# A convolution with two expert layers: the rest of x turned by ScalarE, late masks in PSUM, a new order for the start, and 27 matmuls that nobody reads

## The chip, the core and the metric

The kernel runs on one core of one Trainium2 chip. Time is device microseconds (us) of that core, from a run's start to its end. TensorE is called PE, VectorE DVE, ScalarE ACT, GpSimd POOL and SyncE SP, as in the profile.

## The reference

An x of 2 x 4096 tokens and 192 channels passes through a convolution over 7 tokens, whose weights are a softmax made for each token and head, and then through two layers of the same form.

```python
w = softmax(weight_gen)                       # over the 7 taps, 8 heads
x = einsum('bshk,bskhg->bshg', w, windows(x)) # 8192 tokens x 192
h = x @ moe_w_in                              # 192 x 2048
x = where(h > 0, h, exp(min(h, 0)) - 1) @ moe_w_out      # 2048 x 192
h = x @ moe2_w_in
out = (h * clip(h + 3, 0, 6) / 6) @ moe2_w_out
```

## The kernel before

**Cells.** The 8192 tokens are 16 blocks of 512. For each layer and block the 2048 hidden channels are done in 8 cells of 256, so there are 256 cells, in a fixed order. Cell n has a first product (18 matmuls into the two PSUM banks `hset[n % 2]`) and a second product (into `acca` and `accb`) that is issued three cells later, together with the first product of cell n + 3. Each operand is held as a high part and a rest, so that three products of float32r matmuls (high by high, high by rest, rest by high) stand for one exact product. Most matmuls use 64 of the 128 rows, and two of them run side by side.

**What feeds PE.** Between a cell's first and second product ACT computes relu and exp (`x n`, `y n` in the script below, for the two banks), DVE computes the gate (`X n`, `Y n`), ACT rounds the result to its high part (`R n`), and DVE makes its rest `gl` (`G n`). The operand x of a block is transposed by PE, cast by ACT to `X["h"]` (tile xh), and DVE subtracts to get `X["l"]` (tile xl). Each 64-row half of xh and xl is needed in the other half of the partitions as well. For block 0 ACT copies xh across (`turn`, written `wh2` and `wh3`), and two DMAs on SP copy xl across (`swap`).

**Weight units.** The first layer's weights arrive in 16 units of 128 x 384, `i0` to `i7` for the inner product and `o0` to `o7` for the outer, numbered 0 to 15 as in `units`. A unit k is split into high part and rest by a chain: ACT takes the absolute value into a mask (`B k`), DVE does five steps (`C k.0` to `C k.4`), ACT casts the high part (`H k`), PE sums the parts with four matmuls (`P k`: twice line 191, lines 192 and 193), and ACT casts the sum into the rest (`L k`). The string `masks` says where the mask of a unit lies: x is `aux`, b `accb`, a `acca[0]`, c `acca[1]`, all PSUM; a dash is the SBUF tile tr. The string `sums` says which PSUM bank `P k` writes (d to g are the banks of `hset`).

**Order.** Every engine works its queue in program order. From cell 0 to cell 9 the program order is written out by hand in `SCRIPT`; besides the tokens above, `M n` is cell n on PE, `s1a` to `s1c` and `e1` are the softmax of block 1, `sA`, `sE`, `sB`, `sC` that of block 2, `T1` the transposes of block 1, `J` and `j` its casts and rests, and `wl0`, `wl1` the rests of block 0. POOL multiplies and adds the seven taps of a block once its softmax is there; for block 2 it starts behind `sC` and `T1`. From cell 10 on a planner places the second layer's units by due cells. The cells and their work stay in the same order relative to each other.

Of the kernel before, what the change touches and what calls it, by code (L numbers as in the profile page):

```python
# [8 lines left out]
F32 = mybir.dt.float32  # L9
# [8 lines left out]
def kernel(  # L18
# [20 lines left out]
    nc = tc.nc  # L39
# [18 lines left out]
    UN = 2 * D  # L58
    half = slice(0, HP), slice(HP, P)
# [10 lines left out]
    hset = [[psp.tile([P, 512], F32, name=f"h{i}{k}") for k in range(2)] for i in range(2)]  # L70
# [4 lines left out]
    plus, minus = (cpool.tile([P, P], F32R, name=n) for n in ("plus", "minus"))  # L75
# [6 lines left out]
    WI = [{k: cpool.tile([P, NQ * UN], F32R, tag=f"wi0{k}", name=f"wi0_{k}") for k in "hl"}, None]  # L82
# [245 lines left out]
    def prepare(m, i):  # L328
        X = xts[m, i] = {
            k: act.tile([P, 2, XN], F32R, tag=f"x{k}", name=f"x{k}") for k in "hl"}  # L330
        v = lambda t: t[:, 0].rearrange("p (h c) -> p h c", h=2)
        if m == 0:

            y, yd = ya.pop(i)
            ps = acca if i == 0 else (acca[i % 2], aux)
            for t, src in enumerate([y[:, t, 0:P] for t in range(TM)] + [yd[:, s] for s in range(2)]):
                for h, p in enumerate(half):
                    nc.tensor.transpose(ps[h][:, t * HP:(t + 1) * HP], src[p], ident[p, p])  # L338
            parts = [(ps[h][:, 0:XN // 2], (lambda h: lambda t: v(t)[:, h])(h)) for h in range(2)]
        else:  # L340
            parts = [(zin.pop(i)[:, 0:XN], lambda t: t[:, 0])]

        def cast(k):
            src, w = parts[k]
            nc.scalar.copy(w(X["h"]), src)  # L345

        def turn(a):
            nc.scalar.copy(X["h"][half[1 - a], 1], X["h"][half[a], 0].bitcast(F32))

        def rest(k):  # L350
            src, w = parts[k]
            nc.vector.tensor_tensor(w(X["l"]), src, w(X["h"]).bitcast(F32), op=ALU.subtract)

        def swap(keys, put):
            for k in keys:
                for a in range(2):
                    put(X[k][half[1 - a], 1].bitcast(F32), X[k][half[a], 0].bitcast(F32))

        def split():
            for k in range(len(parts)):  # L360
                cast(k)
            for k in range(len(parts)):
                rest(k)
            swap("hl", lambda o, t: later(1 if (m, i) == (0, 2) else 2, o, t))
        split.cast, split.turn, split.rest, split.swap = cast, turn, rest, swap
        return split

# [144 lines left out]
    def matmuls(n):  # L512

        if n >= len(cells):
            if n - LAG < len(cells):
                whole_second_product(n - LAG)
            return  # L520
        b0, b1, a0, a1 = (second_product(n - LAG, k, b) for b in (1, 0) for k in range(2))
        gg.pop(n - LAG, None)
        l0, l1 = first_product(n, 0), first_product(n, 1)
        x1 = first_product(n + 1, 1)[:2] if n >= EARLY - 1 else []
        l1 = l1[2:] if n >= EARLY else l1
        if n < BOOT:
            rows = [(0, a0), (6, b0), (10 if n >= LAG else 0, l0)], [(0, l1), (9, a1), (15, b1), (19, x1)]
            if n >= EARLY:
                rows = rows[0], [(0, l1), (7, x1), (9, a1), (15, b1)]
        else:  # L530
            rows = [(0, b0), (4, a0), (10, l0)], [(0, l1), (7, b1), (11, x1), (13, a1)]
        plan = [
            (s + j, k, op) for k, runs in enumerate(rows) for s, ops in runs for j, op in enumerate(ops)]
        seen = [added.pop(i) for i in range(3, NB) if n == prep[0, i] - 1]
        for _, k, (o, w, r, st, sp, wait, tell) in sorted(plan, key=lambda e: e[:2]):
            mm = nc.tensor.matmul(o, w, r, start=st, stop=sp).ins  # L536
            if wait:
                tc.add_manual_dep(mm, told[wait].name, SYNC)
            elif seen and k and not tell and o in acca:
                tc.add_manual_dep(mm, seen.pop().name, SYNC)  # L540
            if tell:
                note = nc.sync.nop().ins
                tc.add_manual_dep(note, mm.name, SYNC)
                told[tell] = note
                if now > 2 and tell[1] == 1:

                    transfers(1 + k + (now < NQ))
# [47 lines left out]
    def later(n, out, in_):  # L595

        if now is None or now >= len(cells) or now < BOOT and n == 0:
            nc.sync.dma_start(out, in_)
        else:
            waiting.append((now + n, out, in_))  # L600

    def transfers(count):
        for _ in range(count):
            k = next((k for k, w in enumerate(waiting) if w[0] <= now), None)
            if k is None:
                return
            nc.sync.dma_start(*waiting.pop(k)[1:])

    class Stream:
# [21 lines left out]
    BOOT = 10  # L631
    units = [(u[0], 0, int(u[1]), k) for k, u in enumerate("i0 i1 i2 i3 o0 i4 o1 i5 o2 i6 o3 i7 o4 o5 o6 o7".split())]
    banks = {"x": aux, "b": accb, "a": acca[0], "c": acca[1], "d": hset[0][0], "e": hset[0][1], "f": hset[1][0], "g": hset[1][1]}
    masks, sums = "xxbaccxcx----ccc", "xxbfbedgfedxcxxx"
    made = {}
    SCRIPT = """
        s1a B2 B1 C2.0 e1 C1.0 wh0 s1b wh1 wh2 wl0 s1c wh3 wl1 C2.1 B4 M0 C1.1 B3 C2.2 C4.0 H2 C1.2 C4.1 H1
        C1.3 C3.0 C1.4 C4.2 P1 x0 C3.1 C4.3 C3.2 L1 M1 C4.4 y0 C2.3 X0 B5 C2.4 B6 Y0 P2 x1 C5.0 C6.0 y1 C3.3
        C6.1 X1 L2 M2 H3 C3.4 R0 Y1 C5.1 P3 H4 C6.2 x2 G0 P4 y2 C5.2 C6.3 L3 C5.3 L4 M3 C6.4 C5.4 X2 B7 B8
        Y2 R1 C8.0 C7.0 H5 C8.1 H6 P5 C7.1 x3 C8.2 G1 P6 L5 B9 B10 C7.2 L6 M4 C8.3 H7 sA C10.0 sE X3 y3 C7.3  # L640
        C10.1 C9.0 H8 C8.4 R2 C7.4 Y3 P7 x4 C9.1 C10.2 P8 C9.2 L7 G2 H10 T1 L8 C10.3 y4 M5 C9.3 X4 C9.4 J
        C10.4 sB B12 H9 j B11 R3 Y4 P9 B13 sC C11.0 C12.0 G3 P10 L9 x5 C11.1 C12.1 C11.2 L10 M6 C13.0 H11
        C12.2 C13.1 H12 C11.3 x6 C13.2 C11.4 C13.3 R4 C12.3 C13.4 P11 y5 C12.4 X5 P12 G4 H13 L11 L12 Y5 B14
        X6 M7 R5 C14.0 C14.1 x7 G5 y6 X7 C14.2 P13 H14 C14.3 Y6 L13 M8 C14.4 y7 R6 Y7 B15 G6 x8 P14 R7 C15.0
        X8 L14 M9 C15.1 C15.2 H15 C15.3 C15.4 x9 G7 y8 P15 y9 Y8 X9 L15 Y9 R8 G8
    """

    groups = [("io"[n % 2], 1, n // 2) for n in range(2 * NQ)]
# [22 lines left out]
    with tc.manual_schedule():  # L671
        nc.vector.memset(three, 3.0)
        nc.scalar.activation(warm, three, AF.Exp)
        def make(k):
            made[k] = Unit(*units[k])
# [15 lines left out]
            s()  # L691
        u.p5(aux)
        u.p6()
        for s in c0[5:]:
            s()
        c1, split = attention(1), {0: prepare(0, 0)}

        def products(n):
            nonlocal now
            if n:  # L700
                trail(n - 1)
            now = n
            if n == 2:
                blk[2] = load_block(2)
                for k in range(RAWS + 8, len(units)):
                    make(k)
            matmuls(n)
            if n == begin[2]:
                for s in softmax.pop(2):
                    s()  # L710
# [15 lines left out]
        def special(t):  # L726
            if t == "T1":
                split[1] = prepare(0, 1)
            elif t in ("s1a", "e1", "s1b"):
                c1.pop(0)()  # L730
            elif t == "s1c":
                for s in c1:
                    s()
            elif t == "J":
                split[1].cast(0)
                split[1].cast(1)
            elif t == "j":
                split[1].rest(0)
                split[1].rest(1)
                split[1].swap("hl", nc.sync.dma_start)  # L740
            elif t[:2] == "wh":
                k = int(t[2])
                (split[0].turn if k > 1 else split[0].cast)(k % 2)
            elif t[:2] == "wl":
                split[0].rest(int(t[2]))
                if t == "wl1":
                    split[0].swap("l", nc.sync.dma_start)
                    for k in range(8, RAWS + 8):
                        make(k)
            else:  # L750
                if t == "sA":
                    softmax[2] = attention(2)
                softmax[2].pop(0)()
# [6 lines left out]
        for t in SCRIPT.split():  # L760
            if t[0] == "C":
                k, p = t[1:].split(".")
                getattr(made[int(k)], "s" + p)()
            elif t[0] in plain and t[1:].isdigit():
                plain[t[0]](int(t[1:]))
            else:
                special(t)
# [65 lines left out]
```

## Time and profile before

| | us |
|---|---|
| median of the runs before | 1227.36 |
| lowest run | 1226.69 |
| the profiled execution, its own time | 1227.44 |
| its span, first to last instruction | 1225.6 |
| PE busy | 1188.1 (97%) |
| DVE busy | 944.3 (77%) |
| ACT busy | 856.4 (70%) |
| POOL busy | 417.6 (34%) |

The page of the profile gives busy time by engine. A row of the timeline gives the start in us, the duration in us, the engine, the line, the operation, output and inputs, how many instructions are merged, and in brackets the idle time in front and what ended it. A row of the windows gives the busy time of each engine in a stretch and the granted PE clock as a share of the full one.

### The profile page before, as it was taken

How to read it: one execution, taken by the hardware profiler on the slowest of the kernel's cores; microseconds unless marked ns; L12 is line 12 of the kernel's file. 1: busy time of each engine (PE TensorE's matmuls, PEld its weight loads, DVE VectorE, ACT ScalarE, POOL GpSimd, SP SyncE). 2: the span in 40 equal slices, each digit the busy share in tenths (PEclk: the TensorE clock that was granted, in tenths of full speed). 3: DMA queues.
4: the chain of work that ended last, by engine and by line, in shares of the span. 5: the costliest groups of instructions: out<-in, count | busy, mean ns of one | idle time of the engine just before them, and what ended most of it. 6: DMA issues, size and time to landing. Idle time of an engine off the chain costs nothing.

```text
span 1225.6 us, 25362 instructions
## 1 busy us (share of the span) xinstructions
PE 1188.1 (97%) x10146; PEld 941.7 (77%) x10146; DVE 944.3 (77%) x1223; ACT 856.4 (70%) x1339; POOL 417.6 (34%) x234
## 2 busy tenths in 40 slices
PE   2979999999999999999999999999999999999998
PEld 1647787777778777778788888888888888888886
DVE  7897999999999999998777666666666666666664
ACT  3858788888888888888886666556665555666654
POOL 7582778777778877777000000000000000000000
PEclk9989999999999999999999999999999999999999
DMA  9421122221122222121121111111101111111110
GB/s 207 120 63 62 40 88 89 89 79 65 39 83 89 89 88 69 41 68 53 54 64 52 28 40 53 52 40 53 46 27 46 53 53 40 53 36 30 53 40 27
DMA packets 33414, 75.42 MB, mean 62 GB/s; under 512 B 4372, under 2 KB 17042, under 8 KB 33296
## 3 DMA queue, kind: packets, MB, share of 16 engines
q1 hardware_dynamic: 33152, 73.60, 21.0%
q8 instruction: 80, 1.31, 0.5%
q14 instruction: 38, 0.31, 0.1%
q10 hardware_dynamic: 144, 0.20, 0.0%
HBM read 36.43 MB, written 12.58 MB: 40 GB/s over the span
## 4 chain that ended last, share of the span: by engine, by line
PE 91%; DVE 2%; ACT 0%; DMA 0%; issue 0%; SPq 0%
PE h L536 42%; PE acca L536 28%; PE accb L536 19%; DVE gl L567 1%; PE acca L338 1%; PE acca L432 0%; DVE r L573 0%; PE acca L504 0%; DVE boot L185 0%; PE accb L504 0%; DVE tr L174 0%; DMA xl<-xl 0%; ACT gh L563 0%; PE aux L191 0%; DVE tr L185 0%
## 5 line engine op out<-in xcount | busy, mean ns | idle before, releaser
L536 PE MATMUL h<-xl,wi_h 64*128 64x512 f32 x1536 | 563.2, 395 | 4.4 <-DMA xl<-xl 4.4
L536 PE MATMUL h<-xh,wi_h 64*128 64x512 f32 x1536 | 565.3, 396 | 2.0 <-ACT xh L345 1.5
L536 PE MATMUL h<-xh,wi_l 64*128 64x512 f32 x1536 | 567.1, 396 | 0.1
L536 PE MATMUL acca<-gh,wo 64*128 64x512 f32 x2024 | 558.3, 394 | 0.1
L567 DVE TENSOR_TENSOR gl<-r,gh 128x1024 fp32r<-128x1024 f32 x256 | 394.3, 1540 | 62.7 <-ACT gh L563 61.6
L536 PEld LDWEIGHTS acca<-gh,wo 64*128 64x128 f32 x2024 | 373.5, 185 | 48.5 <-issue 1.6
L559 ACT ACTIVATE r<-h,three 128x512 f32<-128x512 f32 x256 | 176.3, 689 | 222.2 <-PE h L536 112.4
L536 PE MATMUL accb<-gh,wo 64*128 64x512 f32 x1012 | 319.9, 395 | 0.6 <-ACT wo L198 0.6
L536 PE MATMUL acca<-gl,wo 64*128 64x512 f32 x1012 | 317.8, 393 | 1.3 <-DVE gl L567 1.2
L536 PE MATMUL accb<-gl,wo 64*128 64x512 f32 x1012 | 317.3, 393 | 0.3 <-DVE gl L567 0.3
L536 PEld LDWEIGHTS h<-xl,wi_h 64*128 64x128 f32 x1536 | 282.8, 186 | 40.1 <-DMA xl<-xl 5.1
L536 PEld LDWEIGHTS h<-xh,wi_h 64*128 64x128 f32 x1536 | 283.0, 186 | 38.9 <-ACT xh L345 1.7
L536 PEld LDWEIGHTS h<-xh,wi_l 64*128 64x128 f32 x1536 | 282.9, 186 | 35.4 <-ACT wi_l L198 0.5
L576 DVE SCALAR_TENSOR_TENSOR r<-r,h 128x512 f32<-128x512 f32 x256 | 175.8, 687 | 161.1 <-ACT r L559 160.1
L563 ACT CAST gh<-r 128x1024 fp32r<-128x1024 f32 x256 | 266.6, 1042 | 13.3 <-DVE r L573 12.5
L536 PEld LDWEIGHTS acca<-gl,wo 64*128 64x128 f32 x1012 | 186.9, 185 | 26.0 <-DVE gl L567 2.8
L536 PEld LDWEIGHTS accb<-gl,wo 64*128 64x128 f32 x1012 | 186.9, 185 | 23.8 <-DVE gl L567 0.8
L573 DVE SCALAR_TENSOR_TENSOR r<-r,h 128x512 f32<-128x512 f32 x256 | 172.9, 676 | 37.5 <-ACT r L557 36.6
L536 PEld LDWEIGHTS accb<-gh,wo 64*128 64x128 f32 x1012 | 185.0, 185 | 21.6 <-ACT wo L198 0.9
L290 POOL TENSOR_TENSOR tmp<-xt,wt 128x768 f32<-128x768 f32 (+1 forms) x95 | 189.8, 1998 | 6.2
L556 ACT ACTIVATE r<-h 128x512 f32<-128x512 f32 x256 | 152.7, 596 | 49.6 <-PE acca L536 29.0
L557 ACT ACTIVATE r<-r 128x512 f32<-128x512 f32 x256 | 162.0, 633 | 8.1
(158 smaller groups left out, 757.5 us busy)
## 6 DMA issues: line engine op xcount, KB each, us to landing
xt<-in_x_dram SPq DMA_DIRECT2D x14, 960.0 KB, 5.7
xl<-xl SPq DMA_DIRECT2D x64, 192.0 KB, 2.9
xh<-xh SPq DMA_DIRECT2D x62, 192.0 KB, 2.7
z<-z SPq DMA_DIRECT2D x16, 384.0 KB, 2.3
zin<-z SPq DMA_DIRECT2D x16, 384.0 KB, 3.0
out_dram<-ot SPq DMA_DIRECT2D x15, 384.0 KB, 2.3
raw<-in_moe_w_out_dram SPq DMA_DIRECT2D x12, 384.0 KB, 3.1
raw<-in_moe_w_in_dram SPq DMA_DIRECT2D x12, 192.0 KB, 3.4
```

Source lines behind the costliest of these rows:

```text
L290: eng.tensor_tensor(o.rearrange("p t (h g) -> p t h g", g=G), xk, wk.rearrange("p (t h) g -> p t h g", h=H), op=ALU.mult)
L338: nc.tensor.transpose(ps[h][:, t * HP:(t + 1) * HP], src[p], ident[p, p])
L536: mm = nc.tensor.matmul(o, w, r, start=st, stop=sp).ins
L556: nc.scalar.activation(r, h, AF.Relu, scale=-1.0)
L557: nc.scalar.activation(r, r, AF.Exp, scale=-1.0)
L559: nc.scalar.activation(r, h, AF.Relu, bias=three)
L563: nc.scalar.copy(gg[n][0], rs[n])
L567: nc.vector.tensor_tensor(gl, rs.pop(n), gh.bitcast(F32), op=ALU.subtract)
L573: nc.vector.scalar_tensor_tensor(r, r, -1.0, h, op0=ALU.add, op1=ALU.max)
L576: nc.vector.scalar_tensor_tensor(r, r, 6.0, h, op0=ALU.min, op1=ALU.mult)
```

## The change

Four things are edited. The two DMAs that copy the rest of x of block 0 across the partitions are replaced by two ACT copies, `wz0` and `wz1`, at places of their own in the script. The masks of units 11 and 12 move from SBUF to PSUM, 13 and 15 from `acca[1]` to `aux`; the sums of units 11 to 15 move from `aux` and `acca[1]` to banks of `hset`. The script is written anew, with the same tokens otherwise. A new function `spin` issues matmuls of 384 columns whose result nobody reads: 18 behind the sum of unit 0 and in front of block 0's transposes, 9 behind cell 0.

```diff
-        def turn(a):
-            nc.scalar.copy(X["h"][half[1 - a], 1], X["h"][half[a], 0].bitcast(F32))
+        def turn(a, k="h"):
+            nc.scalar.copy(X[k][half[1 - a], 1], X[k][half[a], 0].bitcast(F32))
...
-    masks, sums = "xxbaccxcx----ccc", "xxbfbedgfedxcxxx"
+    masks, sums = "xxbaccxcx--xcxcx", "xxbfbedgfedgfdfd"
     made = {}
     SCRIPT = """
-        s1a B2 B1 C2.0 e1 C1.0 wh0 s1b wh1 wh2 wl0 s1c wh3 wl1 C2.1 B4 M0 C1.1 B3 C2.2 C4.0 H2 C1.2 C4.1 H1
-        C1.3 C3.0 C1.4 C4.2 P1 x0 C3.1 C4.3 C3.2 L1 M1 C4.4 y0 C2.3 X0 B5 C2.4 B6 Y0 P2 x1 C5.0 C6.0 y1 C3.3
-        C6.1 X1 L2 M2 H3 C3.4 R0 Y1 C5.1 P3 H4 C6.2 x2 G0 P4 y2 C5.2 C6.3 L3 C5.3 L4 M3 C6.4 C5.4 X2 B7 B8
-        Y2 R1 C8.0 C7.0 H5 C8.1 H6 P5 C7.1 x3 C8.2 G1 P6 L5 B9 B10 C7.2 L6 M4 C8.3 H7 sA C10.0 sE X3 y3 C7.3
-        C10.1 C9.0 H8 C8.4 R2 C7.4 Y3 P7 x4 C9.1 C10.2 P8 C9.2 L7 G2 H10 T1 L8 C10.3 y4 M5 C9.3 X4 C9.4 J
-        C10.4 sB B12 H9 j B11 R3 Y4 P9 B13 sC C11.0 C12.0 G3 P10 L9 x5 C11.1 C12.1 C11.2 L10 M6 C13.0 H11
-        C12.2 C13.1 H12 C11.3 x6 C13.2 C11.4 C13.3 R4 C12.3 C13.4 P11 y5 C12.4 X5 P12 G4 H13 L11 L12 Y5 B14
-        X6 M7 R5 C14.0 C14.1 x7 G5 y6 X7 C14.2 P13 H14 C14.3 Y6 L13 M8 C14.4 y7 R6 Y7 B15 G6 x8 P14 R7 C15.0
-        X8 L14 M9 C15.1 C15.2 H15 C15.3 C15.4 x9 G7 y8 P15 y9 Y8 X9 L15 Y9 R8 G8
+        s1a B2 B1 C2.0 e1 C1.0 wh0 s1b wh1 wh2 wl0 s1c wh3 C1.1 wl1 C2.1 B3 C1.2 wz0 C3.0 C2.2 B4 C1.3 wz1
+        M0 C2.3 H1 C4.0 H2 C3.1 C4.1 x0 C1.4 C4.2 P1 C3.2 C4.3 C3.3 L1 M1 C4.4 B6 X0 B5 H3 C5.0 y0 C6.0 C5.1
+        C2.4 x1 Y0 P2 C6.1 y1 X1 C5.2 R0 C6.2 C5.3 C3.4 L2 M2 Y1 H4 H6 G0 P3 x2 P4 y2 C6.3 C5.4 L3 X2 L4 M3
+        H5 C6.4 B7 Y2 B8 sA R1 C7.0 C8.0 B10 C7.1 x3 P5 C8.1 C7.2 y3 X3 P6 G1 L5 L6 B9 H7 C7.3 M4 R2 C8.2
+        C10.0 C7.4 C9.0 C10.1 C9.1 x4 C10.2 C9.2 Y3 H8 sE C8.3 H10 P7 X4 R3 C8.4 G2 P8 L7 sB T1 L8 M5 J
+        C10.3 C9.3 sC y4 C9.4 j H9 G3 B12 B11 x5 C11.0 C10.4 Y4 P9 C12.0 P10 L9 C11.1 R4 C12.1 C11.2 C12.2
+        L10 M6 C11.3 y5 C12.3 C11.4 H11 X5 B13 Y5 x6 C12.4 C13.0 H12 P11 G4 B14 P12 L11 R5 C13.1 X6 L12 M7
+        y6 C13.2 C14.0 C13.3 x7 Y6 C13.4 H13 G5 P13 y7 C14.1 L13 X7 M8 B15 R6 C14.2 Y7 x8 C14.3 C15.0 C14.4
+        H14 G6 P14 y8 C15.1 L14 X8 M9 R7 C15.2 C15.3 Y8 x9 C15.4 G7 H15 P15 y9 X9 L15 Y9 R8 G8
     """
...
         u.p5(aux)
         u.p6()
+
+        def spin(count):
+            for _ in range(count):
+                nc.tensor.matmul(hset[1][1][:, 0:UN], plus, WI[0]["h"][:, 0:UN], start=True, stop=True)
+
+        spin(18)
         for s in c0[5:]:
...
             matmuls(n)
+            if n == 0:
+                spin(9)
...
+            elif t[:2] == "wz":
+                split[0].turn(int(t[2]), "l")
             elif t[:2] == "wl":
                 split[0].rest(int(t[2]))
                 if t == "wl1":
-                    split[0].swap("l", nc.sync.dma_start)
                     for k in range(8, RAWS + 8):
                         make(k)
```

## Rows read from the trace of the kernel before

**Rows 1.** Windows: busy us by engine, granted clock, DMA share, GB/s.
```profile
18.70:34.00 15.30, 8.50 (x34) 4.53 (x34) 11.71 (x28) 6.88 (x13) 11.52 (x9) 1.00 1.07 236
34.00:70.00 36.00, 35.17 (x237) 23.85 (x236) 34.32 (x59) 28.00 (x58) 19.48 (x12) 1.00 0.41 125
70.00:81.20 11.20, 4.00 (x8) 1.90 (x8) 11.20 (x13) 5.09 (x9) 10.73 (x7) 0.76 0.05 23
...
150.00:200.00 50.00, 50.00 (x438) 39.97 (x436) 47.26 (x56) 42.01 (x68) 40.62 (x22) 1.00 0.31 96
```

**Rows 2.** Timeline of PE, from unit 0's sum to the start of cell 2.
```profile
11.96 0.52 PE L193 MATMUL aux<-boot,plus 128*128 128x384 f32 x1
18.70 0.48 PE L338 MATMUL acca<-ident,y 64*128 64x64 f32 x4 [6.22 <-DVE y L303]
...
30.65 1.22 PE L536 MATMUL h<-xl,wi_h 64*128 64x512 f32 x4 [4.42 <-DMA xl<-xl]
...
37.64 0.33 PE L193 MATMUL accb<-boot,plus 128*128 128x384 f32 x1
37.90 0.50 PE L536 MATMUL h<-xh,wi_h 64*128 64x512 f32 x2
```

**Rows 3.** Timeline of PE, starts of cells 6 to 10 and of sums.
```profile
64.46 0.50 PE L536 MATMUL h<-xh,wi_h 64*128 64x512 f32 x1
...
76.89 0.69 PE L193 MATMUL aux<-boot,plus 128*128 128x384 f32 x1 [4.71 <-DVE boot L185]
78.97 1.65 PE L191 MATMUL acca<-f,ident 128*128 128x384 f32 x2 [1.39 <-DVE boot L185]
...
81.22 0.79 PE L536 MATMUL h<-xh,wi_h 64*128 64x512 f32 x1
...
83.08 0.49 PE L536 MATMUL h<-xh,wi_h 64*128 64x512 f32 x1
...
88.90 0.50 PE L536 MATMUL acca<-gh,wo 64*128 64x512 f32 x1
...
93.55 0.91 PE L191 MATMUL aux<-f,ident 128*128 128x384 f32 x2
...
94.74 0.50 PE L536 MATMUL acca<-gh,wo 64*128 64x512 f32 x1
...
101.27 0.49 PE L536 MATMUL accb<-gh,wo 64*128 64x512 f32 x1 [0.63 <-ACT wo L198]
```

**Rows 4.** Timeline of DVE, idle times and single steps.
```profile
23.07 0.55 DVE L352 TENSOR_TENSOR xl<-acca,xh 128x384 fp32r<-128x384 f32 x1
...
30.02 0.55 DVE L174 TENSOR_SCALAR accb<-f 128x384 uint32<-128x384 uint32 x1
33.21 0.69 DVE L573 SCALAR_TENSOR_TENSOR r<-r,h 128x512 f32<-128x512 f32 x1 [2.63 <-ACT r L557]
...
41.00 2.50 DVE L567 TENSOR_TENSOR gl<-r,gh 128x1024 fp32r<-128x1024 f32 x1
...
49.25 1.21 DVE L567 TENSOR_TENSOR gl<-r,gh 128x1024 fp32r<-128x1024 f32 x1
...
52.10 0.35 DVE L162 TENSOR_SCALAR tr<-tr 128x384 f32<-128x384 f32 x1
...
65.59 3.62 DVE L165 TENSOR_SCALAR tr<-tr 128x384 uint32<-128x384 uint32 x2
...
74.66 0.54 DVE L169 SCALAR_TENSOR_TENSOR f<-raw,acca 128x384 uint32<-128x384 uint32 x1
75.13 1.71 DVE L185 SCALAR_TENSOR_TENSOR boot<-early_l,tr 128x384 fp32r<-128x384 uint32 x1
```

**Rows 5.** Timeline of POOL, first product of block 2.
```profile
62.87 1.72 POOL L290 TENSOR_TENSOR y<-xt,wt 128x768 f32<-128x768 f32 x1 [15.89 <-PE accb L536]
```

**Rows 6.** Timeline of ACT, the two copies of xh across the partitions.
```profile
22.01 1.67 ACT L348 CAST xh<-xh 64x768 fp32r<-64x768 f32 x2
```

**Rows 7.** Windows of 2 us, the stretch behind PE's long wait.
```profile
76.00:78.00 2.00, 0.69 (x1) 0.29 (x1) 2.00 (x3) 1.67 (x4) 1.92 (x2) 0.50 0.00 0
```

## The prediction

> **What bounds the kernel now.** I read the windows first [rows 1]. From 150 us on PE is busy for all of every 50 us, with 438 matmuls in each such stretch. Nothing in the change touches that part, so it can only move as a whole: the question is how early cell 10 begins, and every us that the start saves or loses stays in the result. Cell 10 starts at 101.27 us now [rows 3].
>
> In front of that I looked for time in which PE doesn't work or works slowly. There are three places. From 18.7 to 34 us PE is busy for 8.50 of 15.3 us [rows 1]. Its timeline shows a wait of 4.42 us for the DMA of xl, with the end of cell 0 only at 30.65 + 1.22 = 31.87 us [rows 2], and DVE idle for 2.63 us as a result [rows 4]. From 34 to 70 us PE has 35.17 of 36 us and DVE 34.32 [rows 1]: both are nearly full. From 70 to 81.2 us PE has 4.00 of 11.2 us while DVE is busy throughout [rows 1]; PE waits 4.71 and 1.39 us for DVE's last step of units 11 and 12 [rows 3], and behind that the granted clock is 0.50, the lower of PE's two levels [rows 7].
>
> Why DVE is late there is seen in its own rows: two mask steps of 384 elements on the SBUF tile tr take 3.62 us at 65.59, and the last step of a unit with its mask in tr takes 1.71 us, while POOL works on block 2 from 62.87 on [rows 4, 5]. The same step without POOL takes 0.35 us, and with the mask in PSUM 0.54 us while POOL is running [rows 4].
>
> **Prices.** DVE goes from 23.07 to 30.02 us in 15 PSUM steps, so one costs 0.463 us from start to start (its duration of 0.55 overlaps by 0.09) [rows 4]. A gate, 0.69 long, then costs 0.60. A `gl` costs 2.4 us while POOL works and 1.13 without it (durations 2.50 and 1.21) [rows 4]. A last step with its mask in SBUF costs 1.63 us beside POOL, as a PSUM step without it. For softmax instructions and mask steps in SBUF without POOL I take 0.30 each (0.35 less the overlap) [rows 4]. On PE a whole cell is 93.55 - 88.90 = 4.65 us and a unit's sum 94.74 - 93.55 = 1.19 at the higher clock [rows 3]; a sum at the lower is 81.22 - 78.97 = 2.25 [rows 3]. Cells 0 to 2, with a first product alone (18 of some 39 matmuls), are half a cell, 2.3 us.
>
> **Rest of x by ScalarE.** Two turns cost 1.67 us of ACT, 0.83 each [rows 6]. They stand behind the turns of xh (which end at 23.68) and two mask openings of half as many columns. The openings are at most 0.83 each by the same row; I take 0.45. So xl is complete between 25.3 us (turns alone) and 27.0; I take 26.3. Four matmuls of cell 0 are left then, 1.22 us as before [rows 2], and cell 0 ends at 27.0 to 27.5 us instead of 31.87. SP's queue loses two DMAs that waited for DVE, so the weight loads behind them leave a little earlier. Nobody waits for those in this stretch, so I cost that at nothing.
>
> **The 18 matmuls in front.** They can start when unit 0's sum ends at 12.48 us, and PE has nothing else until 18.70 [rows 2]. Each has the shape of line 193's matmul: 0.52 us at the lower clock, 0.33 at the higher [rows 2]. That makes 5.9 to 9.4 us, an end between 18.4 and 21.9. The durations overlap, and after the wait at 78.97 the clock was back 4.1 us later (a first pair of 0.79 us at 81.22, one of 0.49 at 83.08) [rows 3], so I take an end near 18.7 and a cost of nothing. At worst the transposes come 3.2 us late. What they can give is cell 0 and unit 1 at the higher clock.
>
> **The 9 matmuls behind cell 0** take 2.7 us at the higher clock and 4.7 at the lower, from 27.0 us on. Unit 1's sum stands behind them on PE. It needs DVE's C1.4, the twelfth PSUM step after 23.07, at 28.63. So cell 1 starts at 27.0 + 2.7 + 1.2 = 30.9 and ends at 33.2. The next sum needs C2.4: 23.07 + 21 steps (9.72) + one gate (0.6) = 33.4 us. The nine are covered by this wait.
>
> **The new order, by DVE's queue.** I add up what stands in it, always with the prices above, and put PE's cells beside it.
>
> - From 33.4: three gates, five steps, `G0` beside POOL: 39.9. PE: sum 2, cell 2 at 34.6 (37.90 before [rows 2]) to 36.9, two sums, cell 3 at 39.3 to 44.0, two sums, cell 4 at 46.4.
> - Eight steps, three gates, two softmax instructions, `G1` without POOL (block 1 done): 47.1. Cell 4 wants `G1` 0.8 us after its start, so it isn't held, and ends at 51.1.
> - Seven steps, four short ones, two gates: unit 8's last step ends at 52.8 and sum 8 at 54.0; the transposes of block 1 (0.48 for four at the lower clock [rows 2]; 0.6 for twelve) follow, and cell 5 runs from 54.6 to 59.3. DVE goes on with `G2`, four softmax instructions and two short steps to 55.7. That is `sC`, and POOL starts block 2 there, not at 62.87.
> - C9.4 beside POOL 1.63, `j` 0.93, `G3` 2.4, one step, C10.4 1.63: 62.8. Sum 9 ends at 60.5 and PE waits 2.3 us for C10.4. Cell 6 starts at 64.0 against 64.46 [rows 3]. So the lead of 3.3 us at cell 2 is used up, because the work of units 11 and 12 and the softmax of block 2 also lie ahead of DVE's later steps, and DVE is the bound.
> - Three gates, nine steps: C12.4 ends at 68.7; one step and `G4`: 71.6. PE: cell 6 to 68.7, two sums, cell 7 at 71.05 instead of 81.22, to 76.05 (5.0, with matmuls of cell 8 taken in).
> - Five steps, two gates: C13.4 at 75.1; `G5`: 77.5. PE: one sum, cell 8 at 77.25 instead of 88.90 [rows 3].
> - Five steps, two gates: C14.4 at 81.0, wanted at 81.9. `G6`: 83.4, wanted at 83.85. Four steps, two gates: C15.4 at 86.5, wanted at 87.7. PE is the bound again, by 0.3 to 1.2 us.
>
> From cell 8 to cell 10 nothing differs from before (12.37 us [rows 3]), so cell 10 starts at 89.6 us, 11.6 earlier. The gain is almost all at the wait in front of cell 7 and the lower clock behind it; units 11 to 15 as PSUM masks make it.
>
> The Trainium skill speaks against this edit: "VectorE: DVE Perf Modes", section "Why PSUM operands drop a tier", says that a PSUM operand takes an fp32 instruction out of the faster two-port mode. By that alone units 11 and 12 lose three steps of 0.2 us each (0.35 against 0.55 [rows 4]), 1.2 us, and the time would be 1228.6. The rows at 65.59 and 74.66 [rows 4] decide otherwise while POOL is running. The Trainium skill's "SBUF — State Buffer", section "Who interferes with whom", has the reason: a DVE instruction with at most one SBUF input and outside that mode doesn't contend with POOL.
>
> **Sums in the banks of hset.** L11 to L14 on ACT must read them before the next cell writes there. Cell 7's first writes need L11, done 0.5 us after sum 11, and ACT has 0.6 us or more to spare; I take nothing, at most 0.5 us for each of cells 7 to 9.
>
> **The sum.** The profiled execution took 1227.44 us, 0.08 above the median of the runs. 1227.44 - 11.6 = 1215.8 us.
>
> **Rivals.** (A) POOL holds DVE longer. A hold can last one whole POOL instruction, 1.72 us [rows 5], in front of DVE's own time: 2.85 for a `gl` and 2.2 for C9.4 and C10.4. With `G3` to `G6` that is 4 x 0.45 + 2 x 0.55 = 2.9 us more, of which 0.3 is spare: 1218.4. For it speaks that POOL begins right at C9.4; against it that the `gl` at 41.00 took 2.50. (B) DVE wins at `sC` and C9.4, `G3` and C10.4 run as without POOL: 2 x 1.17 + 1.27 = 3.6 us earlier, of which PE can use the 2.3 us of its wait in front of sum 10: 1213.5. (C) The spins don't lift the clock, the change doesn't do what it says. Then the nine end at 32.2, sum 1 at 34.4, cell 1 at some 37.4, and cell 2 starts at 38.6 instead of 34.6. DVE's X1 waits for cell 1 just as long, C10.4 slips by 4.0 us, and the time is 1219.8. Against it: PE works from 12.48 without a pause, as it did when the clock came back at 83.08. (D) Slower than before: PE idles 2.3 us in front of sum 10, the clock falls there as it did by 76 to 78 us [rows 7], and the waits for `gl` in cells 6 to 9 keep it low. A cell then costs 9.3 us instead of 4.65. The return at 83.08 cost half of 4.1 us; the gain is gone when PE works over 23 us at the lower level. Against it: the wait that brought the level down was twice as long, 4.71 us.
>
> **How the numbers follow.** Chances: the forecast 0.48, A 0.20, B 0.15, C 0.12, D 0.05. A to C all lie within 1213.5 to 1219.8; with the ends of the unknown prices (the cell starts behind hset's banks, 1.5 us; the spins' lateness, of which the wait for C2.4 covers all but 1 us) the range is 1211.5 to 1221.5. A measurement of this kernel can tell 2% from no change, 24.5 us; more than that could be gained only if more than PE's two gaps went: 0.02. Within 2%: 0.94. Slower by more: 0.04.
>
> **What would show it.** In the profile after, cell 0 should end near 27 us with no wait for a DMA, its matmuls at 0.4 us; PE should wait for DVE some 2 us in front of sum 10; cell 7 should start near 71 and cell 10 near 90; no granted clock under 1 between 60 and 100 us; steps of units 11 to 15 near 0.55 us. A gain much above 14 us, or cell 10 after 95, makes this wrong.

## The result and the profile after

The changed kernel takes 1214.52 us (median; 1213.84 to 1215.17) against 1227.36 us before: a ratio of 0.9895, with a 95% interval of 0.9876 to 0.9915. One of the four runs before took 2097.70 us and is left out. A second set of runs (e12) gave 1214.11 against 1228.16, 0.9886 (0.9871 to 0.9901). So the kernel is about 1% quicker: clear of the noise, and within the 2% for which the prediction gave 0.94. The profiled execution took 1214.76 us with a span of 1213.0, so 12.7 us less than the profiled execution before. 1215.8 was predicted.

The windows after, same stretches and columns as [rows 1]:

```profile
18.70:34.00 15.30, 12.83 (x61) 8.62 (x61) 12.83 (x31) 10.90 (x20) 12.39 (x10) 0.67 1.04 283
34.00:70.00 36.00, 33.80 (x226) 23.56 (x226) 35.83 (x68) 31.27 (x64) 24.36 (x15) 1.00 0.31 99
70.00:81.20 11.20, 11.20 (x85) 8.24 (x83) 10.75 (x17) 8.65 (x17) 10.81 (x6) 1.00 0.01 2
150.00:200.00 50.00, 50.00 (x438) 39.96 (x436) 46.52 (x58) 41.05 (x67) 40.60 (x21) 1.00 0.25 72
```

From 70 to 81.2 us PE is now busy throughout, with 85 matmuls instead of 8, at a clock of 1.00 instead of 0.76. From 150 us on PE's part of the row is as before. In the first stretch PE is busier, but 9 of its 61 instructions are matmuls that nobody reads, and the clock is 0.67. The 1.00 of the same stretch before [rows 1] is no higher clock (see the last section).

PE's timeline, which answers to [rows 2, 3]: unit 0's sum, the 18, the transposes, the end of cell 0, the nine, sums 1 and 2, cell 2, sum 10, the starts of cells 6 to 10.

```profile
12.09 0.52 PE L193 MATMUL aux<-boot,plus 128*128 128x384 f32 x1
12.41 3.93 PE L697 MATMUL h<-wi_h,plus 128*128 128x384 f32 x18
18.76 0.34 PE L338 MATMUL acca<-ident,y 64*128 64x64 f32 x4 [2.42 <-DVE y L303]
...
25.81 1.22 PE L536 MATMUL h<-xl,wi_h 64*128 64x512 f32 x4 [0.19 <-ACT xl L348]
26.96 3.25 PE L697 MATMUL h<-wi_h,plus 128*128 128x384 f32 x9
30.01 1.23 PE L191 MATMUL aux<-f,ident 128*128 128x384 f32 x2
...
35.15 0.91 PE L191 MATMUL accb<-f,ident 128*128 128x384 f32 x2 [1.24 <-DVE boot L185]
...
36.34 0.50 PE L536 MATMUL h<-xh,wi_h 64*128 64x512 f32 x2
...
62.17 0.91 PE L191 MATMUL h<-f,ident 128*128 128x384 f32 x2 [0.70 <-DVE r L573]
...
63.38 0.49 PE L536 MATMUL h<-xh,wi_h 64*128 64x512 f32 x1
...
70.21 0.49 PE L536 MATMUL h<-xh,wi_h 64*128 64x512 f32 x1
...
76.50 0.49 PE L536 MATMUL acca<-gh,wo 64*128 64x512 f32 x1
...
82.34 0.50 PE L536 MATMUL acca<-gh,wo 64*128 64x512 f32 x1
...
88.88 0.50 PE L536 MATMUL accb<-gh,wo 64*128 64x512 f32 x1 [0.63 <-ACT wo L198]
```

Cell 0 ends at 25.81 + 1.22 = 27.03 us, where it ended at 31.87. But at cell 2 the lead is 37.90 - 36.34 = 1.6 us, and at cell 6 it is 1.1. Cell 7 starts at 70.2 instead of 81.2 and cell 10 12.4 us earlier than before. That is the whole difference of the spans (1225.6 - 1213.0 = 12.6) but for 0.2.

DVE's rows, which answer to [rows 4]: a wait in the new order, then the last steps of units 9 and 10 (masks in SBUF), a step of unit 11 (mask in PSUM), and the rests `gl`.

```profile
33.14 0.57 DVE L162 TENSOR_SCALAR acca<-acca 128x384 f32<-128x384 f32 x1 [2.37 <-ACT acca L158]
...
56.66 0.55 DVE L185 SCALAR_TENSOR_TENSOR boot<-early_l,tr 128x384 fp32r<-128x384 uint32 x1
...
58.07 1.64 DVE L567 TENSOR_TENSOR gl<-r,gh 128x1024 fp32r<-128x1024 f32 x1
...
60.09 1.43 DVE L185 SCALAR_TENSOR_TENSOR boot<-early_l,tr 128x384 fp32r<-128x384 uint32 x1
...
62.51 0.55 DVE L165 TENSOR_SCALAR aux<-aux 128x384 uint32<-128x384 uint32 x1
...
73.45 2.37 DVE L567 TENSOR_TENSOR gl<-r,gh 128x1024 fp32r<-128x1024 f32 x1
...
79.25 1.21 DVE L567 TENSOR_TENSOR gl<-r,gh 128x1024 fp32r<-128x1024 f32 x1
```

POOL's first product of block 2, for [rows 5], and on ACT the second turn of xl and the cast of unit 1's rest (L1), for [rows 6]:

```profile
56.97 1.65 POOL L290 TENSOR_TENSOR y<-xt,wt 128x768 f32<-128x768 f32 x1 [10.78 <-issue]
```
```profile
24.92 0.83 ACT L348 CAST xl<-xl 64x768 fp32r<-64x768 f32 x1
...
31.63 0.48 ACT L198 CAST wi_l<-aux 128x384 fp32r<-128x384 f32 x1 [3.30 <-PE aux L193]
```

POOL begins 5.9 us earlier than before and works on through all of unit 11's and 12's steps. These take about 0.55 us each all the same, with their masks in PSUM.

The granted clock, in the columns of [rows 7], around cell 0:

```profile
14.00:16.00 2.00, 2.00 (x13) 2.00 (x12) 1.86 (x5) 0.00 (x0) 1.84 (x3) 1.00 0.73 151
...
18.00:20.00 2.00, 0.68 (x8) 0.40 (x8) 1.93 (x6) 0.89 (x2) 1.92 (x3) 1.00 0.71 183
20.00:22.00 2.00, 0.93 (x6) 0.70 (x8) 1.93 (x7) 1.86 (x5) 0.07 (x1) 0.65 0.96 307
22.00:24.00 2.00, 1.52 (x8) 0.79 (x6) 2.00 (x5) 1.94 (x4) 1.49 (x1) 0.50 1.04 295
...
28.00:30.00 2.00, 2.00 (x7) 2.00 (x7) 2.00 (x5) 0.33 (x1) 1.92 (x2) 0.50 1.09 290
30.00:32.00 2.00, 2.00 (x9) 1.26 (x10) 0.78 (x2) 0.37 (x1) 1.92 (x2) 0.79 1.21 258
```

The 18 end at 16.34 us, 2.42 us ahead of the transposes. The clock is at 0.50 by the time cell 0 runs, and back only during sum 1. So cell 0 and the nine are at the lower level. This end varies from one execution to another: in e8 below, with the same 27 matmuls, the nine took 1.71 us instead of 3.05, so the clock was back during them.

### The profile page after: what moved, and what is told of

It reads as the page before. It is cut to its first block, busy times and chain, and to the rows that moved or that the text cites. A ratio compares the mean times of both kernels' runs of the same rounds, so it can differ in the third digit from the quotient of the medians.

```text
span 1213.0 us, 25422 instructions
## 1 busy us (share of the span) xinstructions
PE 1190.2 (98%) x10173; PEld 947.6 (78%) x10173; DVE 934.1 (77%) x1223; ACT 857.5 (71%) x1341; POOL 418.1 (34%) x234
## 4 chain that ended last, share of the span: by engine, by line
PE 92%; DVE 4%; DMA 2%; SPq 1%; ACT 0%; issue 0%; DVEq 0%; ACTq 0%
PE h L536 43%; PE acca L536 28%; PE accb L536 19%; DVE gl L567 1%; DMA xt<-in_x_dram 1%; DVE r L573 1%; SPq L598 1%; PE acca L338 1%; DMA raw<-in_moe_w_out_dram 1%; PE acca L432 0%; DVE boot L185 0%; PE acca L504 0%; PE h L191 0%; DVE f L169 0%; DMA early_h<-in_moe_w_in_dram 0%
```

## The experiments

Starts of cells in the profiled execution of each kernel (us, PE's timeline), with the median time and the median before of the same chip:

| kernel | 1 | 3 | 6 | 7 | 10 | time | before |
|---|---|---|---|---|---|---|---|
| before | 34.0 | 42.8 | 64.5 | 81.2 | 101.3 | | 1227.36 |
| after | 31.5 | 41.5 | 63.4 | 70.2 | 88.9 | 1214.52 | 1227.36 |
| e1, no spins | 29.4 | 39.8 | 62.1 | 68.9 | 87.6 | 1213.81 | 1227.99 |
| e2, without the nine | 29.9 | 39.9 | 62.0 | 68.8 | 87.5 | 1213.89 | 1227.99 |
| e3, without the 18 | 30.1 | 40.0 | 62.3 | 69.2 | 87.8 | 1214.25 | 1227.99 |
| e4, 32 in front | 29.6 | 39.5 | 62.3 | 69.1 | 87.8 | 1214.22 | 1227.99 |
| e5, masks 11 and 12 in SBUF | 30.9 | 40.8 | 65.4 | 83.0 | 101.7 | 1226.85 | 1228.31 |
| e6, before with PSUM masks | 33.7 | 42.7 | 64.3 | 71.3 | 94.4 | 1219.22 | 1228.31 |
| e7, xl by DMA | 36.2 | 46.1 | 67.9 | 74.7 | 93.4 | 1218.73 | 1228.31 |
| e8, B5 early | 30.4 | 41.1 | 63.1 | 69.9 | 88.6 | 1214.17 | 1228.31 |
| e9, as e6, B12 behind j | 33.0 | 42.3 | 63.9 | 70.9 | 92.2 | 1218.53 | 1228.16 |
| e10, before with xl by ACT | 29.5 | 39.2 | 60.8 | 77.3 | 99.4 | 1225.89 | 1228.16 |
| e11, no spins, three orders | 30.1 | 41.4 | 62.3 | 69.1 | 87.8 | 1213.56 | 1228.16 |
| e12, after again | 31.4 | 41.3 | 63.0 | 69.9 | 88.6 | 1214.11 | 1228.16 |

**The spins.** Four kernels, edited from the changed one; their outputs don't depend on these matmuls.

```diff
-        spin(18)        # e1 and e3 leave it out; e4 has spin(32)
-            if n == 0:
-                spin(9) # e1 and e2 leave it out
```

> The changed kernel without any of the 27 matmuls that nobody reads. Theory (the gain is made by the PSUM masks and the order behind cell 5; the spins give nothing, and the nine delay the sum of unit 1, behind which ScalarE holds the next mask openings): cell 0 as before at the lower clock, ending near 27.0 us; unit 1's sum starts at 27.9 instead of 30.0, its cast and the mask openings come some 1.4 us earlier, cell 6 at 62 to 63.4, the time 1213 to 1214.5. Rival (the spins raise the clock and so make the early part of the gain): cell 1 at the lower clock, cell 2 some 2 us later than in the changed kernel, DVE late by the same, the time 1216 to 1217.

> The changed kernel with the 18 matmuls in front but without the nine behind cell 0. Theory: the clock has fallen again before cell 0 whatever the 18 do, so this equals the kernel without spins, 1213 to 1214.5. Rival (the nine lift the clock for cell 1): cell 1 and sum 1 at the lower clock, cell 2 1 to 2 us later, 1215.5 to 1216.5.

> The changed kernel with the nine behind cell 0 but without the 18 in front. Theory: the 18 end at 16.3 us, PE then has little to do until 21.4, and the clock is at its lower level in cell 0 with or without them: the time is that of the changed kernel within 0.5 us, 1214 to 1215. Rival (the 18 matter): cell 1 later by 1 us or more, 1215.5 to 1217.

> The changed kernel with 32 in front instead of 18, at the rate that the last of the 18 showed enough to fill the gap up to the transposes at 18.8 us. If the clock falls because the 18 end 2.4 us too early, cell 0 now runs at the higher level (pairs 0.23 us apart), the nine take 1.5 us instead of 3.05, unit 1's sum starts at 28.0, and the time is 1212 to 1213.5. If the transposes alone let it fall, cell 0 is as in the changed kernel and the time is 1214 to 1215; if the 32 reach beyond 18.8 us, the transposes are late and the time is up by as much.

Measured: 1213.81, 1213.89, 1214.25 and 1214.22 us; the ratios are 0.9886 (0.9869 to 0.9903), 0.9887 (0.9870 to 0.9903), 0.9891 (0.9870 to 0.9911) and 0.9889 (0.9873 to 0.9906). The intervals overlap with each other and with the changed kernel's. So the spins gain nothing that these runs can show, and the rival falls in all three. Without the nine, sum 1 starts at 27.7 to 27.8 us instead of 30.0 and cell 10 some 1.3 us earlier in the trace; but e3 and e4, which keep the nine, have cell 10 earlier by 1.1 us as well, so this isn't shown to be theirs. In e4 the gap was filled (the 32 end at 19.92 us, and cell 0 starts when it did), and still cell 0 was at the lower level for its greater part. The windows, then PE's rows:

```profile
20.00:22.00 2.00, 1.05 (x16) 0.60 (x14) 1.93 (x7) 1.94 (x5) 0.04 (x1) 1.00 1.07 239
22.00:24.00 2.00, 1.03 (x6) 0.79 (x6) 2.00 (x6) 1.94 (x4) 1.42 (x1) 0.79 1.08 242
24.00:26.00 2.00, 1.76 (x10) 0.88 (x8) 2.00 (x6) 1.95 (x4) 1.92 (x3) 0.50 1.14 248
```
```profile
21.39 0.50 PE L536 MATMUL h<-xh,wi_h 64*128 64x512 f32 x2 [0.95 <-ACT xh L345]
21.72 0.40 PE L536 MATMUL h<-xh,wi_l 64*128 64x512 f32 x2
23.10 0.75 PE L536 MATMUL h<-xh,wi_h 64*128 64x512 f32 x2 [0.97 <-ACT xh L348]
```

Cell 0's first four matmuls ran at the higher level, then the clock fell in the middle of the cell, where PE waits for the turns of xh. e4's time lies in the range it expected for a cell 0 as in the changed kernel; that the gap in front of the transposes alone lets the clock fall is refuted.

**The place of the masks**, undone in the changed kernel.

```diff
-    masks, sums = "xxbaccxcx--xcxcx", "xxbfbedgfedgfdfd"
+    masks, sums = "xxbaccxcx----xcx", "xxbfbedgfedgfdfd"
-        ... H9 G3 B12 B11 x5 C11.0 C10.4 Y4
+        ... H9 G3 B12 C10.4 B11 x5 C11.0 Y4
```

> The changed kernel with the masks of units 11 and 12 back in SBUF (the tile tr; for its two buffers C10.4 stands one place earlier). Theory (the place of these masks makes the gain): beside POOL, which now works from 57 us on, each of the ten steps is held as at 65 to 80 us in the kernel before, +1.3, 1.3, 1.25, 0.7 and 1.2 us a unit, some 11 us of DVE for both; cell 7 at 78 to 81 instead of 70.2, the clock lower behind it, the time 1222 to 1226. Rival (the order alone makes it): cell 7 before 73, 1214 to 1217.

Measured: 1226.85 us, a ratio of 0.9992 (0.9982 to 1.0002) to the kernel before; no gain is left that shows. DVE's and PE's rows of this run show where it went:

```profile
65.10 3.61 DVE L165 TENSOR_SCALAR tr<-tr 128x384 uint32<-128x384 uint32 x2
68.64 2.20 DVE L169 SCALAR_TENSOR_TENSOR f<-early_l,tr 128x384 uint32<-128x384 uint32 x1
...
72.58 3.58 DVE L174 TENSOR_SCALAR tr<-f 128x384 uint32<-128x384 uint32 x2
76.08 2.15 DVE L185 SCALAR_TENSOR_TENSOR boot<-early_l,tr 128x384 fp32r<-128x384 uint32 x1
```
```profile
78.89 1.65 PE L191 MATMUL h<-f,ident 128*128 128x384 f32 x2 [7.25 <-DVE r L573]
```

Each of these steps on tr takes 1.8 to 2.2 us. PE waits 7.25 us for DVE, and comes back at the lower level (1.65 us for a pair that takes 0.91). The mechanism was as expected, but bigger: the time was 0.9 us above the expected range, and cell 7 came at 83.0 us, not at 78 to 81.

**The masks alone**, in the kernel before. In e6 the mask of unit 12 is written to acca[1] in front of the place where block 1's rests are read there, so xl of block 1 holds other values; the instructions are the same ones. e9 puts B12 behind j.

```diff
-    masks, sums = "xxbaccxcx----ccc", "xxbfbedgfedxcxxx"
+    masks, sums = "xxbaccxcx--xcxcc", "xxbfbedgfedxcxxx"
-        ... j B11 R3 Y4 P9 B13 sC ... M6 C13.0 H11 C12.2 C13.1 H12 C11.3 x6 C13.2 C11.4 C13.3 R4 C12.3 C13.4
+        ... j B11 R3 Y4 P9 sC ... M6 H11 C12.2 H12 C11.3 x6 C11.4 R4 C12.3
-        P11 y5 C12.4 X5 P12 G4 H13 L11 L12 Y5 B14 X6 M7 R5 C14.0 C14.1 x7 G5 y6 X7 C14.2 P13
+        P11 y5 C12.4 X5 P12 G4 L11 L12 B13 C13.0 Y5 B14 C13.1 X6 M7 R5 C13.2 C14.0 C13.3 C13.4 x7 G5 H13 y6 X7 C14.1 P13 C14.2
# e9 in addition
-        sB B12 H9 j B11
+        sB H9 j B12 B11
```

> The kernel before with that part alone: masks of unit 11 in aux and of unit 12 in acca[1], and unit 13 (mask in aux) moved behind the casts of units 11 and 12 in the script; no spins, xl by DMA, the old order otherwise. Theory: cell 6 stays at 64.5 us, C12.4 ends near 70 and cell 7 starts at 72 to 73 instead of 81.2, the clock stays up, 8 to 10 us less: 1218 to 1220. Rival (the early lead is needed as well, or the old order stalls elsewhere): above 1222.

> The kernel before with the masks of units 11 and 12 in PSUM once more, with B12 behind the rests of block 1 in the script, so that these read what they read in the kernel before. Theory (masks alone give some two thirds of the gain): as the first run of this edit, 1218 to 1220.5. Rival (that run was quick because the mask was opened in front of j): 1221 or more.

Measured: 1219.22 us, 0.9929 (0.9906 to 0.9952), and 1218.53 us, 0.9925 (0.9910 to 0.9939). Both lie in the expected ranges. So this edit gives 9 to 10 us without the turn, the spins and the new start: cell 6 stays about where it was (63.9 and 64.3) and cell 7 moves by 10 us. It isn't the place of the masks alone, though: unit 13's five steps, which stood in front of cell 7, now stand behind it, and at 0.46 us each they are 2.3 us of DVE. Their share isn't separated here. They don't make the gain alone: in e5 they stand behind all the steps of units 11 and 12 too (C13.0 at 79.98 us), and cell 7 is late. The place of the sums wasn't run by itself; e9 has the old one, and cell 7 comes early all the same. From cell 7 to cell 10 e9 needs 21.3 us where the changed kernel needs 18.7. The cast of unit 13's rest comes late, since on ACT it stands behind H14, which waits for DVE (ACT's row, then PE's):

```profile
79.90 0.51 ACT L180 CAST wo<-f 128x384 fp32r<-128x384 f32 x1 [2.95 <-DVE f L169]
...
80.73 0.50 PE L536 MATMUL acca<-gh,wo 64*128 64x512 f32 x1 [1.75 <-ACT wo L198]
```

**The rest of x**, undone in the changed kernel (e7), and alone in the kernel before (e10).

```diff
# e7
-        ... C1.2 wz0 C3.0 C2.2 B4 C1.3 wz1
+        ... C1.2 C3.0 C2.2 B4 C1.3
                 if t == "wl1":
+                    split[0].swap("l", nc.sync.dma_start)
# e10
-        ... wh3 wl1 C2.1 B4 M0
+        ... wh3 wl1 wz0 wz1 C2.1 B4 M0
                 if t == "wl1":
-                    split[0].swap("l", nc.sync.dma_start)
```

> The changed kernel with the rest of x of block 0 copied across by the two DMAs again. Cell 0 ends near 31 us instead of 27.0. Theory: unit 1's sum, its cast and the mask openings behind it come some 3 us later and DVE, which has no slack up to cell 6, passes 2 to 4 us of it on: 1216 to 1218. Rival (the copy is hidden, since cell 6 waits for DVE anyway): within 0.7 us of the changed kernel, 1213.5 to 1215.

> The kernel before with the other part alone: the rest of x of block 0 turned by two ACT copies behind wl1, no DMAs; masks, order and the rest as before. Theory (the two parts are worth more together: while units 11 and 12 are held by POOL the early lead is lost in front of cell 7, as with the changed kernel's masks back in SBUF): 1225 to 1228, cell 7 near 80. Rival (the parts add): 4.5 us less than before, 1223 to 1224.

Measured: e7 1218.73 us, 0.9929 (0.9909 to 0.9948), 4.6 us above e12; slightly above the expected 1216 to 1218. e10 1225.89 us, 0.9982 (0.9972 to 0.9991): 2.3 us less than before, within the theory's 1225 to 1228. But cell 7 starts at 77.3 us, not near 80, so the theory's reason fails. The rows say why, DVE's of e7 and then PE's of e10:

```profile
32.71 0.69 DVE L573 SCALAR_TENSOR_TENSOR r<-r,h 128x512 f32<-128x512 f32 x1 [3.11 <-ACT r L557]
...
37.80 0.57 DVE L162 TENSOR_SCALAR acca<-acca 128x384 f32<-128x384 f32 x1 [4.41 <-ACT acca L158]
```
```profile
72.97 0.69 PE L193 MATMUL aux<-boot,plus 128*128 128x384 f32 x1 [4.71 <-DVE boot L185]
...
75.05 1.65 PE L191 MATMUL acca<-f,ident 128*128 128x384 f32 x2 [1.40 <-DVE boot L185]
...
77.29 0.79 PE L536 MATMUL h<-xh,wi_h 64*128 64x512 f32 x1
...
79.16 0.79 PE L536 MATMUL h<-xh,wi_h 64*128 64x512 f32 x1
...
83.59 0.47 PE L536 MATMUL h<-xh,wi_h 64*128 64x512 f32 x1
```

In e7 a late cell 0 stops DVE for 7.5 us, and cell 6 comes at 67.9, later than before. In e10 the lead is 3.7 us at cell 6. The two waits in front of cell 7 are those of before, 4.71 and 1.40 us [rows 3], and the lead comes through them whole: 3.9 us at cell 7. It is lost behind them. Cell 7 runs at the lower level until 83.6 us, for 6.3 us, where before it was back at 83.08, after 1.9 [rows 3]. So 1.9 us of lead are left at cell 10.

**The wait that the new order makes** (e8), and a version without it, without spins and with two more moves (e11).

```diff
# e8 and e11
-        ... C3.3 L1 M1 C4.4 B6 X0 B5 H3 C5.0 y0 C6.0 C5.1 C2.4 x1 Y0 P2 C6.1
+        ... C3.3 C4.4 X0 B5 L1 M1 B6 H3 C5.0 y0 C5.1 C2.4 x1 Y0 P2 C6.0 C6.1
# e11 in addition, and no spins
-        ... P2 C6.0 C6.1 y1 X1 C5.2 R0 C6.2 C5.3 C3.4 L2 M2
+        ... P2 L2 C6.0 C6.1 y1 X1 C5.2 R0 C6.2 C5.3 C3.4 M2
-        ... H9 G3 B12 B11 x5 C11.0 C10.4 Y4 P9
+        ... H9 C10.4 Y4 G3 B12 B11 x5 C11.0 P9
```

> The changed kernel with the mask opening of unit 5 in front of the cast of unit 1's rest on ScalarE (B5 in front of L1; DVE takes C5.1 and C2.4 in front of C6.0). In the trace after, DVE idles 2.37 us for this opening, which stood behind L1, which waits for unit 1's sum. Theory (DVE's queue sets the start of cell 6): C2.4 ends 2 us earlier, cell 6 at 61.5 to 62.5 instead of 63.4, the time 1 to 2 us less, 1212 to 1213.2. Rival (PE's own work from cell 1 on is the bound): no change, 1213.8 to 1214.6.

> The changed kernel without spins, with the mask opening of unit 5 in front of the cast of unit 1's rest, the cast of unit 2's rest right behind its sum, and C10.4 and Y4 in front of G3. Theory (what is left is PE's 0.35 us in front of cell 2's last matmuls and 0.7 us in front of sum 10, and DVE's 2.4 us): cell 6 some 1.5 us earlier, 1212 to 1213.2. Rival (another queue takes each of these waits over): 1213.5 to 1214.5.

> The changed kernel once more, as the reference for the version without spins on the same chip: 1213.8 to 1215.2.

Measured: e8 1214.17 us, 0.9892 (0.9872 to 0.9911); e11 1213.56, 0.9879 (0.9863 to 0.9896); e12 1214.11, 0.9886 (0.9871 to 0.9901). The theory's gain of 1 to 2 us isn't there, and e8's time is its rival's. The rival's reason, PE's own work, isn't what PE's rows show: the wait of 2.37 us goes, but cell 2 then waits for the cast of unit 2's rest on ACT, and cell 3 starts at 41.1.

```profile
37.66 0.97 PE L536 MATMUL h<-xh,wi_l 64*128 64x512 f32 x6 [1.22 <-ACT wi_l L198]
```

e11's time lies in its rival's range as well (another queue takes the waits over): its PE waits 1.74 us for DVE in front of sum 3. It is the lowest median of all. It has 0.55 us less than e12, inside both intervals, so it can't be called faster.

## Why the prediction was right

**What bounds the start, and where the gain is.** Right. Cell 10 starts 12.4 us earlier, and 11.0 of them have appeared by cell 7. That the masks make the greater part is shown from both sides: e5 takes 12.7 us more than e12 (the times before of the two sets differ by 0.15 us), and e9, where unit 13's steps move with the masks, 9.6 less than before. The loss that the prediction priced at 0.35 against 0.55 us a step is outweighed. The price of a PSUM step beside POOL came from [rows 4], and the steps of unit 11 have it (0.55). The Trainium skill's "SBUF — State Buffer", section "Who interferes with whom", says that a DVE instruction with two SBUF inputs, or in a two-port mode, contends with POOL, and that one with at most one SBUF input outside these modes doesn't. The traces agree: in e5 nine of the ten steps of units 11 and 12, all on tr, take 1.1 to 2.2 us beside POOL (the tenth 0.70), and in the changed kernel these ten take 0.54 to 0.55.

One reading was wrong. The second wait of [rows 3], 1.39 us, isn't for unit 12's last step. DVE's rows show that it ended with unit 13's, whose mask lay in acca[1], the bank that sum 12 writes:

```profile
78.38 0.54 DVE L185 SCALAR_TENSOR_TENSOR boot<-raw,acca 128x384 fp32r<-128x384 uint32 x1
78.84 1.70 DVE L185 SCALAR_TENSOR_TENSOR boot<-raw,tr 128x384 fp32r<-128x384 uint32 x1
```

The sum needs unit 12's step, which ends at 80.54, only for its last matmul at 80.74. Also, the 0.35 us of [rows 4] is the price of a mask step; a last step with its mask in SBUF takes 0.55 without POOL (C9.4).

**Rest of x by ScalarE.** The end of cell 0 was right (27.03 against 27.0 to 27.5). What failed is the worth that I gave it. I let the lead be used up by cell 6 and put the gain down to the masks alone. In the new order the turn is worth 4.6 us (e7), in the old one 2.3 (e10). In the new order DVE waits for the openings B5 and B6 on ACT, which stand behind sum 1 and so behind cell 0. In the old one the lead came through to cell 7, and two us of it went there at the lower clock; why the clock came back no earlier than before isn't shown. e9 (1218.53) and everything but the turn (e7, 1218.73) take the same time, so the new order without the turn gives nothing that shows.

**The spins.** The cost of nothing was right, in part by luck. The end was not: 16.34 us instead of 18.7, since the later ones took some 0.15 us each (13 of them between 14 and 16 us) where I had 0.33, a duration and not the time from start to start. Neither cell 0 nor the start of sum 1 was at the higher clock: PE did not work on from 12.48 us without a pause, on which I had set rival C aside. The nine took 3.05 us, close to the 2.7 that I had for the higher level, but at the lower one: a price too high and a clock too low cancelled. So the condition of rival C came true for cell 0 and the nine, and its price did not: e1, which has no spin at all, isn't slower. The Trainium skill's "TensorE: Matmul & The Clock Gate", section "HAM oscillation — how this bites in real kernels", says that waits for DMA between short bursts of matmuls return the clock to the lower level. The 0.50 at 22 to 24 us agrees in kind, but the waits in front of it are for DVE, POOL and ACT, the longest 2.42 us; in e4 the clock fell with no wait above 0.97.

**DVE's queue.** The sum had C2.4 at 33.4 us, and it ended at 35.1. A term was missing, the wait of 2.37 us: C5.0 needs the mask opening B5, which stood behind L1 on ACT, which waited 3.30 us for sum 1. Cells 3 to 5 were 2.2, 2.0 and 1.0 us later than my figures. Against that the prices beside POOL were too high. C9.4 began 0.3 us before POOL and took 0.55 us instead of 1.63. `G0` took 1.63 us, `G3` 1.64, `G4` 1.59, `G6` 1.21 and only `G5` 2.37, where I had 2.4 from start to start. And the wait in front of sum 10 was 0.70 us, not 2.3; C10.4 ended at 61.52, and what PE waited for to 62.17 was the gate behind it (Y4, to 62.12), which reads the bank that sum 10 writes. So cell 6 came at 63.4 against 64.0, and cell 10 at 88.9 against 89.6: two errors of about 2 us that nearly cancel, which is luck. The time came out 1.1 us below the forecast. The mis-sized term is the price of DVE's SBUF work beside POOL, nearer to rival B than to the forecast.

**The others.** The banks of hset cost nothing visible: cells 8, 9 and 10 start at 76.50, 82.34 and 88.88 us, spaced as before [rows 3]. For A and D there is no sign: no `gl` up to cell 10 takes more than 2.37 us, where A has 2.85, and the clock is 1.00 from 34 to 100 us.

## What to carry to other kernels

Short DVE steps that work in SBUF alone can be stretched, beside a busy POOL, to about the length of POOL's instructions (here 1.8 to 2.2 us); with the mask in PSUM they took 0.55. If such steps stand in front of the bound engine, moving the mask to PSUM is worth far more than the slower mode loses (0.35 against 0.55 us without POOL). What a lead at the start is worth depends on what comes behind it, here 2.3 us in the old order and 4.6 in the new one; so run each part alone and each left out, and look up in the trace where a lead goes. Before an engine is kept warm by empty work, find out whether it is what the next stage waits for: here it was not.

## What the hardware showed beyond that

The clock fell without a long pause of PE: between 16.34 us and cell 0 at 21.41 there were twelve transposes and waits of 2.42 us and less, and in e4 it fell in the middle of cell 0, behind waits of 0.97 us and less. And the column of the granted clock shows 1.00 before its first change in a trace, while the matmuls of that stretch have the durations of the lower level (0.52 us for line 193's at 12.09 us and 0.34 for the same one of unit 2 at 36.08), so at the start of a kernel durations have to be read, not that column.
